# Loading attention keys as whole contiguous rows, shifted by half a row, into a single buffer behind the queries

## The chip, the cores and the metric

The kernel runs on one core of one Trainium2 chip. The metric is the device time of one execution in microseconds (us). Engines are named as in the profile: PE is TensorE (PEld its weight loads), DVE is VectorE, ACT is ScalarE, POOL is GpSimd, and SP is SyncE, whose queue issues nearly all DMAs.

## The reference

What is computed is a pooled attention, followed by a routed feed-forward layer.

```
q, k, v: (8 batches, 8 heads, 1152 rows, 64), float32
q_pool = mean of each two successive query rows          # 576 queries a head
attn   = softmax(q_pool @ k.T / sqrt(64));  x = attn @ v # x: (8, 576, 512), heads side by side
score  = x @ w_gate                                      # one a token
for each batch: the 128 tokens with the highest score get
    x += sigmoid(score) * (relu(x @ w1) @ w2)            # w1: 512 x 1024, w2: 1024 x 512
```

## The kernel before

The work is done by the class `_Plain`; the order of every instruction on every engine is written out by hand in `run` (line 1576), and nothing is rearranged afterwards. A second routine, `_any_scores`, stands behind a branch for inputs out of range and isn't taken here.

Heads are taken in 32 pairs, and each pair in two halves of 288 pooled queries, so that the main loop has 64 rounds, h = 0 to 63. In each round PE computes the scores of half h (`scores`, L883: 36 matmuls of 64x64 weights by 288 columns, four of them for each of nine blocks of keys), and then the weighted values of half h - 1 (`weighted`, L901, 36 matmuls). The profile shows each of these matmuls as two records, hence "x72" for a block. ACT takes the exponents of the scores (L890). POOL (L922) and DVE (L927) sum them into the softmax's denominators, and POOL and DVE also gate, divide and rank. Twice in each pair of batches and once in the end the expert layers run on PE in between (L1451, L1326, L1346).

Each of the pairs 1 to 31 (pair 0 is loaded in another way, by `load_first`) is prepared thus:

- `load_pair` issues eight DMAs on SP's queue. The 1152 key rows of a head are cut into 32 runs of 36 rows, one run to a partition. Four "quarters" (two heads by two halves of the 64 numbers of a row) fill the 128 partitions of the tile kb, so that each DMA (L742) fetches 32 x 36 pieces of 32 numbers, 128 bytes each. The queries go the same way into qb (L745). kb has two buffers, as the pool `load` has by default; qb has one.
- `prepare_pair` adds neighbouring queries on POOL (L767, qb to qp), and DVE turns keys (L770, kb to kT) and queries (L774, qp to qT) in blocks of 32 x 32. kT and qT have two buffers each. L770 frees a kb buffer, L767 frees qb.
- `load_values` issues four DMAs (L756), lines of 2,304 bytes, into one of two buffers of v_sb.

A round with even h = 2n issues `prepare_pair` for pair n + 1. The next round, h = 2n + 1, issues on SP in this order: the loads of keys and queries of pair n + 2, the values of pair n + 1, the stores of a finished pair's x (`stored`, L1038), and a piece of the weights in the early rounds. Behind them, at the marks in `units`, come the routing's small DMAs (L1108 to L1111, L1208, L1212, L1283, L1296), and copies of the summed weights, tw (L725, L730). SP takes its queue strictly in order: where one DMA waits for a buffer, all behind it wait too.

At one place the tile kb serves for something else: the routing of batch 6 borrows one for a 128 x 512 block on its way to a transposition (L1292 to L1298).

Of the kernel before, what the change touches and what calls it, by code (L numbers as in the profile page):

```python
# [10 lines left out]
P = 128  # L11
BLK = 32

G = 3
F32 = mybir.dt.float32
# [12 lines left out]
def _any_scores(  # L28
# [450 lines left out]
    pairs = [(b, hp) for b in range(B) for hp in range(NPAIR)]  # L479
    in_pair = [(j, t) for j in range(2) for t in range(NF)] + [(0, NF)]  # L480
    upcoming = load_pair(*pairs[0])
    run(prepare_pair(upcoming))
    preparing = iter(())
    routing = iter(())
# [23 lines left out]
    for n, (b, hp) in enumerate(pairs):  # L508
        pair = upcoming
        run(preparing)  # L510
        if hp == 0:
            x = xpool.tile([P, NT, Dm], F32, name="x")
        for i, (j, t) in enumerate(in_pair):
            now = {"pair": pair, "j": j, "t": t, "x": x}
            advance(now)
            if two is not None and two["t"] == NF and two["pair"]["hp"] == NPAIR - 1:
                run(routing)
                routing = routed(two["pair"]["b"], two["x"])
            one, two = now, one
            if i == 0 and n + 1 < len(pairs):  # L520
                upcoming = load_pair(*pairs[n + 1])
                preparing = prepare_pair(upcoming)
            if n == 0 and i == 0:
                load_weights()
            if i >= 3:
                next(preparing, None)
            next(routing, None)
    for _ in range(2):
        advance(None)
        one, two = None, one  # L530
    run(routing)
    run(routed(B - 1, x))


class _Plain:
# [199 lines left out]
    def load_pair(self, b, hp):  # L735

        nc = self.nc
        kb = self.load.tile([P, self.KB, BLK], F32, name="kb")
        qb = self.load.tile([P, self.QB, 2, BLK], F32, name="qb", bufs=1)
        for j, ds, rows in self.quarters():  # L740
            of = self.k[b, 2 * hp + j, :, ds]
            nc.sync.dma_start(kb[rows, :, :], of.rearrange("(i n) d -> i n d", i=BLK))  # L742
        for j, ds, rows in self.quarters():
            of = self.q[b, 2 * hp + j, :, ds].rearrange("(i m) d -> i m d", i=BLK)
            nc.sync.dma_start(qb[rows, :, :, :].rearrange("i n r d -> i (n r) d"), of)  # L745
        return {"k": kb, "q": qb, "b": b, "hp": hp}

    def load_values(self, pair):
# [12 lines left out]
    def prepare_pair(self, pair):  # L761

        nc = self.nc
        qp = self.load.tile([P, self.QB, BLK], F32, name="qp", bufs=1)
        kT = pair["kT"] = self.load.tile([P, self.S], F32, name="kT")
        qT = pair["qT"] = self.load.tile([P, self.Sp], F32, name="qT")
        nc.gpsimd.tensor_tensor(  # L767
            out=qp[:, :, :], in0=pair["q"][:, :, 0, :], in1=pair["q"][:, :, 1, :], op=ALU.add
        )
        nc.vector.transpose(  # L770
            kT.rearrange("p (c g i) -> p c g i", c=self.NC, i=BLK),
            pair["k"].rearrange("p (g c) d -> p c g d", c=self.NC),
        )
        nc.vector.transpose(qT[:, :], qp.rearrange("p n d -> p (n d)"))  # L774

# [296 lines left out]
    def routed(self, b, part):  # L1072


        nc, ffn, Sp, NT, NF = self.nc, self.ffn, self.Sp, self.NT, self.NF
# [138 lines left out]
        for s0, w in self.slots:  # L1214
# [64 lines left out]
            if b != self.B - 1:  # L1279

                n = P // BLK
# [7 lines left out]
            if b != self.B - 1:  # L1289
                yield True  # L1290
                if b == self.B - 2:
                    moved = self.load.tile([P, self.KB, BLK], F32, name="kb")  # L1292
                else:
                    moved = ffn.tile([P, NT, P], F32, name="pick", bufs=1)
                moved = moved.rearrange("p t n -> p (t n)")[:, 0 : self.Dm]
                nc.sync.dma_start(moved, copy.rearrange("a (j b) m -> (a j) (b m)", b=n))  # L1296
                yield "sums" if b < self.B - 2 else True
                nc.vector.transpose(  # L1298
                    xeT.rearrange("p c (j b) -> p c b j", b=n),
                    moved.rearrange("p (b i c) -> p c b i", b=n, c=self.ND),  # L1300
                )
            else:
                yield mid
                pv = self.banks()[:, 0, :].rearrange("p (c n) -> p c n", n=P)
                of = xe.rearrange("p (n c) -> p c n", c=self.ND)
                for c in range(self.ND):
                    nc.tensor.transpose(pv[:, c, 0:w], of[0:w, c], self.ident[0:w, 0:w])
                nc.scalar.copy(xeT[:, :, 0:w], pv[:, 0 : self.ND, 0:w])
# [451 lines left out]
```

## Time and profile before

| | us |
|---|---|
| timed runs (3) | 689.4, 690.31, 693.59; median 690.31 |
| the profiled execution | 686.07 |
| its span, from the first to the last instruction | 684.3 |
| DVE transposing keys, L770, 31 times | 42.1 in all, 1.357 each |
| POOL adding queries, L767, 31 times | 43.7 in all, 1.410 each |
| DMA traffic in the span | 101.22 MB, 148 GB/s at the mean |

The page gives for each engine its busy time, its share of the span and its instructions. Below that, rows of 40 digits cut the span into equal slices of 17.1 us, in which a digit is the busy share in tenths (9 is 90% or more). The DMA row is the mean busy share of the core's 16 DMA engines; PEclk is the granted clock of TensorE. A queue's row has its packets, its megabytes, and the share of the 16 engines' span that its packets took. The chain of work that ended last is followed back from the last instruction. In its list by time, and in the timeline, a row is: start, duration, engine, line, and what it writes and reads; a number behind x says how many instructions were merged. In the list of DMA issues the columns are what is written and read, the queue, the number of DMAs, kilobytes of each, and the median time in us from issue to landing. On SP's rows the duration is the time that SP spent on issuing. In PE's rows the weights of a block can be loaded a little ahead of its first matmul.

### The profile page before, as it was taken

Reading aid. Unit: us, or ns where it says so; the run is one execution under the profiler, and the core shown is the slowest. Engines: PE = TensorE matmul, PEld = TensorE weight load, DVE = VectorE, ACT = ScalarE, POOL = GpSimd, SP = SyncE. Lnnn points to the kernel's source line nnn. Section 1 sums busy time; section 2 is a strip of 40 time slices with the busy share of each in tenths; the row PEclk is TensorE's granted clock in tenths of the full one; section 3 lists DMA queues with packets and bytes.
Section 4 is the critical chain, followed back from the end, with each engine's and each line's share of the span. In section 5 each row is a group of like instructions: output and inputs, shape, how many; then the busy total and the mean of one; then the engine's idle time right before and its main releaser. Section 6 shows DMA issues by size and latency. Waiting matters only on the chain.

```text
span 684.3 us, 23659 instructions
## 1 busy us (share of the span) xinstructions
PE 676.4 (99%) x9972; PEld 570.0 (83%) x9972; DVE 531.6 (78%) x844; ACT 457.5 (67%) x998; POOL 516.1 (75%) x503
## 2 busy tenths in 40 slices
PE   8999999999999999999999999999999999999996
PEld 6667899999999998786889899777788999877875
DVE  3867888998999886786599976595879989688830
ACT  5677778777877773847777777583877777575220
POOL 4778888889888883866997888383999798559241
PEclk9999999999999999999999999999999999999999
DMA  8888888778768878743878797773787877544311
GB/s 169 161 178 186 200 149 206 162 133 173 153 147 173 170 146 144 211 87 79 227 133 184 128 191 139 141 184 63 156 192 167 148 152 166 117 116 119 81 47 36
DMA packets 396899, 101.22 MB, mean 148 GB/s; under 512 B 377200, under 2 KB 380912, under 8 KB 395504
## 3 DMA queue, kind: packets, MB, share of 16 engines
q1 hardware_dynamic: 395328, 95.13, 67.3%
q0 software_dynamic: 1296, 4.20, 1.9%
q8 instruction: 80, 1.31, 0.8%
q10 hardware_dynamic: 160, 0.30, 0.2%
q14 instruction: 35, 0.29, 0.1%
HBM read 81.97 MB, written 17.62 MB: 146 GB/s over the span
## 4 chain that ended last, share of the span: by engine, by line
PE 96%; DMA 2%; issue 1%; POOL 0%; ACT 0%; POOLq 0%; DVE 0%
PE ps L901 41%; PE ps L883 41%; PE ps L1451 11%; DMA out_dram<-xe,index 1%; PE ps L1326 1%; PE ps L616 1%; DMA out_dram<-lines,index_part 0%; PE ps L850 0%; PE ps L833 0%; ACT p L890 0%; PE ps L1229 0%; POOL xe L1511 0%; PE ps L1131 0%; POOL out_dram L1393 0%; ACT hT L1334 0%
## 5 line engine op out<-in xcount | busy, mean ns | idle before, releaser
L890 ACT ACTIVATE p<-ps 128x576 f32<-128x576 f32 x576 | 320.4, 699 | 3.0 <-PE ps L883 2.9
L922 POOL TENSOR_TENSOR acc<-p 128x576 f32<-128x576 f32 x192 | 275.5, 1462 | 31.4 <-ACT p L890 30.8
L883 PE MATMUL ps<-qT,kT 64*64 64x288 f32 x4608 | 295.5, 403 | 0.6 <-DVE token L637 0.5
L901 PE MATMUL ps<-p,v_sb 64*64 64x288 f32 x4608 | 295.2, 403 | 0.0
L901 PEld LDWEIGHTS ps<-p,v_sb 64*64 64x64 f32 x4608 | 236.3, 133 | 43.6 <-ACT p L890 12.1
L883 PEld LDWEIGHTS ps<-qT,kT 64*64 64x64 f32 x4608 | 230.9, 133 | 49.1 <-ACT p L890 5.1
L927 DVE TRANSPOSE_TENSOR_REDUCE fold<-p 128x54 f32<-128x1728 f32 x64 | 126.1, 1970 | 43.7 <-ACT p L890 43.4
L927 DVE TRANSPOSE_TENSOR_REDUCE fold<-acc 128x54 f32<-128x1728 f32 x64 | 124.9, 1951 | 22.2 <-POOL acc L922 22.1
L909 ACT COPY two<-ps 128x576 f32<-128x576 f32 x64 | 40.8, 637 | 136.6 <-PE ps L901 126.6
L911 POOL TENSOR_TENSOR av<-two 128x288 f32<-128x288 f32 x64 | 51.2, 800 | 80.7 <-ACT two L909 79.1
L990 POOL TENSOR_TENSOR prod<-avb,w_gate 128x288 f32<-128x288 f32 x64 | 51.1, 800 | 0.2
L767 POOL TENSOR_TENSOR qp<-qb 128x576 f32<-128x576 f32 x31 | 43.7, 1410 | 6.2 <-DMA qb<-in_q_dram 3.4
L980 DVE STREAM_TRANSPOSE avb<-av 128x288 f32<-128x288 f32 x64 | 28.8, 451 | 24.4 <-POOL av L911 24.0
L770 DVE STREAM_TRANSPOSE kT<-kb 128x1152 f32<-128x1152 f32 x31 | 42.1, 1357 | 0.0
L967 ACT ACTIVATE sums<-total,tiny 32x18 f32<-32x18 f32 x124 | 38.2, 308 | 1.9
L1027 POOL TENSOR_TENSOR x<-avb,rec 128x576 f32<-128x576 f32 x30 | 34.8, 1159 | 0.0
L1178 DVE SCALAR_TENSOR_TENSOR pick<-sc_row,gate_sc,before 128x128 f32<-128x128 f32 (+1 forms) x40 | 29.7, 744 | 1.4
L952 ACT COPY groups<-sum 32x36 f32<-32x36 f32 x124 | 27.2, 220 | 1.6
L1049 DVE TENSOR_REDUCE red<-prod 128x9 f32<-128x288 f32 x64 | 27.7, 433 | 0.1
L1459 ACT COPY s<-ps 128x256 f32<-128x256 f32 (+1 forms) x27 | 11.4, 447 | 20.9 <-PE ps L1451 20.9
L937 DVE TENSOR_REDUCE sum<-fold 128x18 f32<-128x108 f32 x64 | 21.9, 342 | 2.2
L1459 ACT COPY hT<-ps 128x512 f32<-128x512 f32 (+1 forms) x15 | 7.8, 544 | 23.3 <-PE ps L1451 21.3
(136 smaller groups left out, 493.1 us busy)
## 6 DMA issues: line engine op xcount, KB each, us to landing
kb<-in_k_dram SPq DMA_DIRECT2D x124, 144.0 KB, 4.3
qb<-in_q_dram SPq DMA_DIRECT2D x124, 144.0 KB, 3.7
v_sb<-in_v_dram SPq DMA_DIRECT2D x124, 144.0 KB, 3.6
tw<-tw SPq DMA_DIRECT2D x10, 1024.0 KB, 7.2
out_dram<-x SPq DMA_DIRECT2D x128, 72.0 KB, 3.2
lines<-row_rank SPq DMA_DIRECT2D x7, 640.0 KB, 4.1
w<-in_moe_w_dram SPq DMA_DIRECT2D x8, 512.0 KB, 5.1
tw<-tw SPq DMA_DIRECT2D x8, 512.0 KB, 4.7
```

Of the source, the lines that this page charges most:

```text
L767: nc.gpsimd.tensor_tensor(out=qp[:, :, :], in0=pair["q"][:, :, 0, :], in1=pair["q"][:, :, 1, :], op=ALU.add)
L770: nc.vector.transpose(kT.rearrange("p (c g i) -> p c g i", c=self.NC, i=BLK), pair["k"].rearrange("p (g c) d -> p c g d", c=self.NC),)
L883: nc.tensor.matmul(sc[keys, j, 0:n], lhsT=pair["kT"][rows, c * P + keys.start : c * P + keys.stop], rhs=pair["qT"][rows, qs], start=True, ...
L890: nc.scalar.activation(p[:, c // G, c % G, :, :], sc[:, :, 0:n], AF.Exp, scale=self.scale)
L901: nc.tensor.matmul(av[j * self.D : (j + 1) * self.D, e, 0:n], lhsT=half["pair"]["v"][keys, j, c, :], rhs=half["p"][keys, c // G, c % G, j, :],
L909: nc.scalar.copy(two[:, :, :], av[:, :, 0:n])
L911: nc.gpsimd.tensor_tensor(out=half["av"][:, :], in0=two[:, 0, :], in1=two[:, 1, :], op=ALU.add)
L922: nc.gpsimd.tensor_tensor(out=acc[:, u, :], in0=units[:, 0, u, :], in1=units[:, 1, u, :], op=ALU.add)
L927: nc.vector.tensor_reduce(fold[:, a, :], of.rearrange("p u (m d) -> p (u m) d", d=BLK), AX.X, ALU.add, apply_transpose=True,)
L967: self.nc.scalar.activation(tot[rows, :], pair["total"][:, j * self.QB : (j + 1) * self.QB], AF.Identity, bias=self.tiny[0:BLK, 0:1],)
L990: self.nc.gpsimd.tensor_tensor(out=pair["prod"][:, ns, :], in0=pair["avb"][:, ns, :], in1=self.w_gate[:, hp : hp + 1, :].broadcast_to([P, ...
L1451: nc.tensor.matmul(args[0], lhsT=args[1], rhs=args[2], start=k == 0, stop=k == n - 1)
```

## The change

Keys: each DMA fetches, for each of the 32 partitions of its quarter, one contiguous line of 36 x 64 - 32 = 2,272 numbers, 9,088 bytes, in place of 36 pieces of 32. For the second half of a row the line begins 32 numbers later, so that in both cases the 32 numbers that are wanted of key row n stand at the beginning of a 64-number slot n of the tile; the other 32 are fetched and not used. The tile kb is twice as wide, 64 numbers for 32, and has one buffer instead of two: the same room. L770 reads the first 32 of each 64.

Order: in `load_pair` the four query DMAs are issued ahead of the four key DMAs. On all other engines the order of instructions is what it was. On SP the first key DMA of a pair now waits for DVE's transposition of the previous pair's keys; the first query DMA waits, as before, for POOL's addition of the previous pair's queries.

The tile that batch 6 borrows takes the new shape and the one buffer, too.

```diff
@@ def load_pair(self, b, hp):
-        kb = self.load.tile([P, self.KB, BLK], F32, name="kb")
+        kb = self.load.tile([P, self.KB, self.D], F32, name="kb", bufs=1)
         qb = self.load.tile([P, self.QB, 2, BLK], F32, name="qb", bufs=1)
-        for j, ds, rows in self.quarters():
-            of = self.k[b, 2 * hp + j, :, ds]
-            nc.sync.dma_start(kb[rows, :, :], of.rearrange("(i n) d -> i n d", i=BLK))
         for j, ds, rows in self.quarters():
             of = self.q[b, 2 * hp + j, :, ds].rearrange("(i m) d -> i m d", i=BLK)
             nc.sync.dma_start(qb[rows, :, :, :].rearrange("i n r d -> i (n r) d"), of)
+        n = self.KB * self.D - BLK
+        for j, ds, rows in self.quarters():
+            of = self.k[b, 2 * hp + j].rearrange("(i n) d -> i (n d)", i=BLK)
+            nc.sync.dma_start(
+                kb[rows, :, :].rearrange("i n d -> i (n d)")[:, 0:n], of[:, ds.start : ds.start + n]
+            )
@@ def prepare_pair(self, pair):
         nc.vector.transpose(
             kT.rearrange("p (c g i) -> p c g i", c=self.NC, i=BLK),
-            pair["k"].rearrange("p (g c) d -> p c g d", c=self.NC),
+            pair["k"][:, :, 0:BLK].rearrange("p (g c) d -> p c g d", c=self.NC),
         )
@@ in routed(self, b, part):
                 if b == self.B - 2:
-                    moved = self.load.tile([P, self.KB, BLK], F32, name="kb")
+                    moved = self.load.tile([P, self.KB, self.D], F32, name="kb", bufs=1)
```

Here BLK is 32, D is 64, KB is 36 and P is 128; `quarters` yields the head j, the half ds of a row, and the 32 partitions.

## The prediction

> **What bounds the kernel now.** I read the page's table of engines first, then the 40 slices, the chain of work that ended last, the DMA issues, and last the timeline of SyncE's queue (SP), DVE, POOL and PE's weight loads, pair by pair.
>
> ```profile
> PE 676.4 (99%) x9972; PEld 570.0 (83%) x9972; DVE 531.6 (78%) x844; ACT 457.5 (67%) x998; POOL 516.1 (75%) x503
> PEclk9999999999999999999999999999999999999999
> DMA  8888888778768878743878797773787877544311
> q1 hardware_dynamic: 395328, 95.13, 67.3%
> ```
>
> TensorE is busy for 676.4 of 684.3 us, at full clock in every slice. The DMA engines are busy 70 to 90% for most of the run; that is no bound until PE is seen waiting for them. An ordinary stretch of the chain:
>
> ```profile
> 102.24 4.36 PE ps L883 x72
> 106.61 4.38 PE ps L901 x72
> 110.99 4.37 PE ps L883 x72
> 115.36 4.37 PE ps L901 x72
> ```
>
> From 19 to 634 us the chain is PE alone: a block of scores (L883), a block of weighted values (L901), 4.36 to 4.38 us each with no gap, whether the slice's DMA digit is 8 or 4. A block that doesn't stretch runs at its own rate. The few longer ones (4.55 at 40.80, 4.47 and 4.52 from 389.75) are worth 0.5 us together, and ScalarE's exponents ended their idle. No PE line in the list of waits names a DMA.
>
> [...]
>
> So a load costs time only if a block finds its operand late. The loads, and the place where they are tightest:
>
> ```profile
> kb<-in_k_dram SPq DMA_DIRECT2D x124, 144.0 KB, 4.3
> qb<-in_q_dram SPq DMA_DIRECT2D x124, 144.0 KB, 3.7
> v_sb<-in_v_dram SPq DMA_DIRECT2D x124, 144.0 KB, 3.6
> tw<-tw SPq DMA_DIRECT2D x10, 1024.0 KB, 7.2
> ```
> ```profile
> 359.14 7.13 SPq L742 DMA_DIRECT2D kb<-in_k_dram  x4
> 366.37 4.54 SPq L745 DMA_DIRECT2D qb<-in_q_dram  x4
> 371.01 2.07 SPq L756 DMA_DIRECT2D v_sb<-in_v_dram  x4
> ```
> ```profile
> 354.93 1.41 POOL L767 TENSOR_TENSOR qp<-qb 128x576 f32<-128x576 f32 x1
> ```
> ```profile
> 357.08 1.36 DVE L770 STREAM_TRANSPOSE kT<-kb 128x1152 f32<-128x1152 f32 x1
> 358.37 0.72 DVE L774 STREAM_TRANSPOSE qT<-qp 128x576 f32<-128x576 f32 x1
> ...
> 374.32 1.36 DVE L770 STREAM_TRANSPOSE kT<-kb 128x1152 f32<-128x1152 f32 x1
> ```
> ```profile
> 363.04 4.36 PEld L883 LDWEIGHTS ps<-qT,kT 64*64 64x64 f32 x72
> ...
> 376.32 3.70 PEld L901 LDWEIGHTS ps<-p,v_sb 64*64 64x64 f32 x64 [0.20 <-ACT p L890]
> ```
>
> Keys and queries are turned at 357.08, done at 359.09, wanted by PE at 363.04: 3.95 us in hand. Over all 31 pairs the same rows give 3.5 us or more, but for 1.3 (the first, done at 21.6), 0.70 and 0.68 (L770 at 342.87 and 508.30). The values are tighter: issued last on SP, to 373.08, plus 3.6 to land is 376.7, and PE takes them at 376.32. By that count the hand is nothing at 376.32 and 211.16, 0.6 at 541.74, 1.9 to 2.2 at 228.63, 246.11 and 576.69, and over 3 elsewhere; as PE doesn't wait, those landed faster than the median.
>
> **The change part by part.**
>
> *Line length.* A pair's keys were 4 x 32 x 36 = 4,608 lines of 128 bytes; they become 128 lines of 9,088. Bytes rise from 31 x 4 x 147,456 = 18.3 MB to 31 x 4 x 290,816 = 36.1 MB, the mean rate from 148 to (101.2 + 17.8) / 684.3 = 174 GB/s; today's slices reach 227. The 142,848 short packets took at most about 18.6 ns each (67.3% x 16 x 684.3 us over q1's 395,328), 24 points of the share; less if short ones are cheaper than the mean. The trace has no 284 KB load. Its landing lies between v_sb's 3.6 us (144 KB in long lines) and tw's 7.2 (1,024 KB), by size 3.6 + 140 x 3.6 / 880 = 4.2, which I take, as the size is nearest v_sb's; today 4.3 at the median, 8.6 at most. SP's issue takes 914 ns at the median for 1,152 lines, 426 for v_sb's 64 (311 at least). I take 0.43: 1.7 us a pair instead of 3.7, with 0.31 and 0.91 as ends. On the path: 0, PE waits for no load.
>
> *Order.* The queries' DMAs go ahead of the keys' on the one SP queue. Their wait for L767 was there before, since qb had one buffer already; now keys, too, stand behind it and behind 4 x 0.86 = 3.4 us of issues. Queries come earlier where L767 isn't the wait. POOL's 3.4 us of waits for qb should shrink; POOL is off the path: 0.
>
> *One buffer for kb.* A pair's first key DMA now waits for the L770 of the pair before. In the stretch shown: L767 ended at 356.34, queries issue from 359.14 to 362.6; L770 ended at 358.44, so the new wait is over before SP gets there; keys issue to 364.3 and land at 368.5, against a want of 374.32. Done for all pairs, the wait is last on SP only twice, where DVE comes late out of routing work (L770 at 269.51 and 434.92): 2.8 and 3.4 us, and what SP issues behind it, values first, then x's stores and the routing's small DMAs, goes 0.1 us later than before (values at 272.6 and 438.0 for 272.46 and 437.87), with over 25 us in hand. From the keys' last issue to their L770 there are 8.75 us at the least (pair 2), 9 to 9.6 in four more, 10 or more elsewhere, for a landing of 4.2. Where L767 is late and SP waits, values come up to 2 us later (73.5 for 71.57) with 11 in hand; in the tight places they come earlier, by 4.0 (211.16), 6.7 (376.32) and 5.0 us (541.74). On the path: 0. If this cover were gone, a late landing would stop DVE at L770, the folds queued behind it, and then PE.
>
> [...] If one buffer meant no overlap, 31 landings of 4.2 us would come out, 130 us. The rows above leave the load room, and the sum has 0.
>
> *The transpose's reading.* L770 reads the same 1,152 elements in runs of 32, now with a gap behind each. No row has just this. Below: 1.36 us as now, since the runs stay whole and successive runs lay apart already; nothing would make it quicker. Above: L1298, which picks elements four apart, 1.11 us for 512, so 2.5 for 1,152. I take 1.36. The upper end puts 36 us on DVE; from 100 to 200, where it is busy for 91.85, it would reach 98.4.
>
> *Start and end.* Pair 1's queries are issued from 5.67 instead of 10.45, its keys from about 10.5 instead of 5.67, landing near 17 before L770's 19.58. The kb tile borrowed at 639 us only has another shape; its last reader ended at 601.9. Both 0.
>
> Sum: 0. The profiled execution took 686.07 us (span 684.3 and 1.8 around it); the timed runs 689.4, 690.31 and 693.59, so it stands 4.2 below their median. Nothing moves on the profile's scale. The one loose end, the values' hand, can only pull the runs toward their fast end, so I say the lowest of them: 689.4.
>
> **The rivals.**
>
> 1. *Relief makes it faster.* For: values land just in time in three places. Against: PE doesn't wait there. If all that sets the median above the profiled run were such waits, 686.1; with PE's idle of the first 20 us (2.0), 684.1, still only 0.9% under the median.
>
> 2. *DVE reads the wider pitch more slowly.* Against: whole runs. Price at the upper end: 0.45 + 0.47 us in the two pairs with 0.7 in hand, and up to 5.7 pairs x 1.15 = 6.6 in the stretch where DVE is full: 686.07 + 7.5 = 693.6, or 697 on the runs' scale (from 689.4); halfway, 693.
>
> 3. *The long lines hold up SP, and values come late: slower.* Place: the values behind the keys. Point: four key issues take over 1.7 + 4.0 = 5.7 us, after which PE waits at 211.16. Price: if they take 8.7, today's longest four (at 279.25), 7.0 beyond my 1.7, the hands of ten tight pairs run out by 3.0, 1.6, 1.4, 0.8, 0.7, 0.6, 0.4, 0.2 and two noughts, 8.7 in sum: 694.8, or 699 on the runs' scale (690.31 + 8.7), 1.3% slower. For: twice the bytes in a queue that is 67% full. Against: tw's loads of 1,024 KB issue in 0.58 us at the median and land in 7.2.
>
> 4. *The long lines are cut up on the way*, so that one costs what two of today's do. Time as forecast until rival 3's point.
>
> **How the numbers follow.** About 1% is what a measurement of this kernel can tell from no change. Hidden: 0.78, and rival 4 0.04. Rival 2: 0.07, nearly all within 1%. Rival 3: 0.07, slower. Rival 1: 0.04, counted as faster by over 1% for the part that the profile can't show. So 0.04 faster, 0.89 within, 0.07 slower. The range: from 684.1 (rival 1) to 696.0, between rival 2's middle and its end; rival 3 lies above.
>
> **What would show it.** Right: blocks of 4.37 us, PE near 676 busy, about 139,000 packets fewer, q1 near 113 MB, key issues under 0.5 us, landing near 4.2, an SP wait for L770 in a few pairs. Wrong: L770 above 1.4 us, DVE waiting for kb, or a PE wait at L883 or L901 released by L770, L774 or a DMA.

## The result and the profile after

The changed kernel takes 714.1 us at the median of six runs (711.48 to 720.93), the kernel before 691.38 (689.4 to 693.68): a ratio of 1.0331, 95% interval 1.0295 to 1.0366. The forecast was 689.4, "the same", with 696.0 as the upper end of its range. The profiled execution took 711.59 us, with a span of 709.8 where before it was 684.3: 25.5 us more. The lines of after stand three lower in the code: scores L886, weighted values L904, the transpositions L773 and L777, the addition L770, the stores of x L1041; L742 is now the queries and L746 the keys, L759 the values.

The page of after, the rows on engines, DMA and chain, and two groups (the columns of a group: busy us in all and mean ns of one, then the idle time just before them and what ended most of it):

```profile
PE 687.2 (97%) x9972; PEld 564.5 (80%) x9972; DVE 531.6 (75%) x844; ACT 458.0 (65%) x998; POOL 515.4 (73%) x503
DMA  9889899898879887873887988786678989844310
q1 hardware_dynamic: 256448, 112.91, 73.3%
PE 67%; DMA 12%; POOL 8%; SPq 5%; DVE 4%; issue 3%; ACT 2%; POOLq 0%; DVEq 0%; ACTq 0%
L904 PE MATMUL ps<-p,v_sb 64*64 64x288 f32 x4608 | 303.3, 408 | 9.5 <-DMA v_sb<-in_v_dram 9.3
L886 PE MATMUL ps<-qT,kT 64*64 64x288 f32 x4608 | 299.7, 406 | 6.0 <-DVE qT L777 5.4
```

The same two groups before:

```profile
L883 PE MATMUL ps<-qT,kT 64*64 64x288 f32 x4608 | 295.5, 403 | 0.6 <-DVE token L637 0.5
L901 PE MATMUL ps<-p,v_sb 64*64 64x288 f32 x4608 | 295.2, 403 | 0.0
```

The 25.5 us are 14.7 in which PE stands idle (709.8 - 687.2 = 22.6, before 684.3 - 676.4 = 7.9) and 10.8 in which it is busy for longer with the same 9,972 matmuls. The idle time lies at the two waits that the groups name: 9.5 us ahead of L904 (before 0.0), nearly all of it for the values' DMA, and 6.0 ahead of L886 (before 0.6). The same two lines are busy for 8.1 and 4.2 us more (before 295.2 and 295.5); neighbouring groups overlap at their edges, so that the two don't add up to the 10.8. The chain, PE alone before, now runs through DMA and SP's queue for 17% of the span.

The DMA issues of after, and then what SP waited for longest (us in total, times, longest):

```profile
kb<-in_k_dram SPq DMA_DIRECT2D x124, 284.0 KB, 6.6
qb<-in_q_dram SPq DMA_DIRECT2D x124, 144.0 KB, 4.2
v_sb<-in_v_dram SPq DMA_DIRECT2D x124, 144.0 KB, 7.5
out_dram<-x SPq DMA_DIRECT2D x128, 72.0 KB, 5.1
```
```profile
SPq L1041 <- DMA kb<-in_k_dram: 80.9, 105, 2.1
SPq L742 <- POOL qp L770: 44.0, 10, 8.7
```

A key load lands 6.6 us after its issue at the median (before 4.3). But DMAs that did not change land late, too: the values 7.5 us after theirs (before 3.6), the stores of x 5.1 (before 3.2). And the 128 stores on SP's queue waited 105 times for a key load to land, a wait that the trace of before does not have at all; it delays all that SP issues behind them. In all 105, the load that was waited for is the eighth DMA ahead of the store on SP's queue: with four loads of keys, four of values and four stores in this order, a key load has that place. The stores of before:

```profile
out_dram<-x SPq DMA_DIRECT2D x128, 72.0 KB, 3.2
```

What that makes of one pair, first SP's queue in the kernel before, then after:

```profile
123.12 4.14 SPq L742 DMA_DIRECT2D kb<-in_k_dram  x4
127.35 4.24 SPq L745 DMA_DIRECT2D qb<-in_q_dram  x4
131.69 2.58 SPq L756 DMA_DIRECT2D v_sb<-in_v_dram  x4
```
```profile
117.42 5.33 SPq L1041 DMA_DIRECT2D out_dram<-x  x4
...
128.94 4.36 SPq L742 DMA_DIRECT2D qb<-in_q_dram  x4
133.40 2.46 SPq L746 DMA_DIRECT2D kb<-in_k_dram  x4
135.95 1.83 SPq L759 DMA_DIRECT2D v_sb<-in_v_dram  x4
```

The issue of keys takes 2.46 us instead of 4.14, as was meant. Yet SP comes to this pair 5.8 us later than before, and to the values 4.3 us later (135.95 for 131.69). The chain of after shows the rest, values last, and then PE's timeline at this place and at the next such one:

```profile
137.35 7.67 DMA v_sb<-in_v_dram
```
```profile
136.94 4.63 PE L886 MATMUL ps<-qT,kT 64*64 64x288 f32 x72
144.30 6.88 PE L904 MATMUL ps<-p,v_sb 64*64 64x288 f32 x70 [2.73 <-DMA v_sb<-in_v_dram]
...
219.13 6.83 PE L904 MATMUL ps<-p,v_sb 64*64 64x288 f32 x70 [2.18 <-DMA v_sb<-in_v_dram]
...
565.41 6.31 PE L904 MATMUL ps<-p,v_sb 64*64 64x288 f32 x70 [3.19 <-DMA v_sb<-in_v_dram]
```

PE had ended its scores at 141.57 and stopped for 2.73 us, until the values began to be there; the last of their four loads, issued at 137.35, took 7.67 us, to 145.02, and most of the block follows it. The block behind the stop takes 6.88 us instead of 4.63. The stretches around it say why (us, busy time and instructions of PE, PEld, DVE, ACT and POOL, then the granted clock, the DMA share and GB/s):

```profile
144.30:150.00 5.70, 5.55 (x56) 3.60 (x60) 5.59 (x17) 0.06 (x1) 0.95 (x2) 0.70 0.77 129
150.00:155.00 5.00, 5.00 (x86) 3.83 (x81) 4.93 (x10) 3.48 (x7) 1.55 (x3) 1.00 0.99 228
```

The granted clock is 0.70 in the 5.7 us after the stop, and 1.00 thereafter. So this stop costs twice: 2.73 us of standing, and some 2.4 of slow matmuls. The three blocks shown are 6.88 + 6.83 + 6.31 - 3 x 4.5 = 6.5 of PE's 10.8 us of longer busy time (4.5 is 70 records at the rate of a block of 72 in 4.63). The two other stops of over 2 us stand ahead of scores:

```profile
359.38 6.28 PE L886 MATMUL ps<-qT,kT 64*64 64x288 f32 x72 [2.69 <-DVE qT L777]
531.40 4.60 PE L886 MATMUL ps<-qT,kT 64*64 64x288 f32 x72 [2.25 <-DVE qT L777]
```

The first has 1.7 us more of slow matmuls behind it (granted clock 0.73 over these 6.28 us, and 0.75 over each of the blocks at 219.13 and 565.41), which makes 8.2 of the 10.8. The second has none: the granted clock is 1.00 from 531.40 to 536.00, after a stop longer than the 2.18 ahead of 219.13. So a stop of this length does not always cost twice. At 359.38 the chain runs back through POOL to the routing's indirect loads (7.17 us there; 6.7 at the median, before 4.0), so values and keys are not the only loads that came late.

### The profile page after: what moved, and what is told of

The parts are those of the page before. It is cut to its first block, busy times and chain, and to the rows that moved or that the text cites. A ratio compares the mean times of both kernels' runs of the same rounds, so it can differ in the third digit from the quotient of the medians.

```text
span 709.8 us, 23676 instructions
## 1 busy us (share of the span) xinstructions
PE 687.2 (97%) x9972; PEld 564.5 (80%) x9972; DVE 531.6 (75%) x844; ACT 458.0 (65%) x998; POOL 515.4 (73%) x503
## 2 busy tenths in 40 slices
DMA packets 258019, 119.00 MB, mean 168 GB/s; under 512 B 234352, under 2 KB 238064, under 8 KB 252656
## 3 DMA queue, kind: packets, MB, share of 16 engines
q1 hardware_dynamic: 256448, 112.91, 73.3%
## 4 chain that ended last, share of the span: by engine, by line
PE 67%; DMA 12%; POOL 8%; SPq 5%; DVE 4%; issue 3%; ACT 2%; POOLq 0%; DVEq 0%; ACTq 0%
PE ps L904 30%; PE ps L886 25%; PE ps L1454 11%; POOL acc L925 4%; DMA v_sb<-in_v_dram 4%; DMA kb<-in_k_dram 2%; DMA out_dram<-xe,index 2%; DVE fold L930 2%; SPq L742 2%; SPq L746 2%; ACT p L893 1%; DMA row<-total 1%; PE ps L1329 1%; DMA xe<-out_dram,index 1%; POOL x L1030 1%
## 5 line engine op out<-in xcount | busy, mean ns | idle before, releaser
L904 PE MATMUL ps<-p,v_sb 64*64 64x288 f32 x4608 | 303.3, 408 | 9.5 <-DMA v_sb<-in_v_dram 9.3
L886 PE MATMUL ps<-qT,kT 64*64 64x288 f32 x4608 | 299.7, 406 | 6.0 <-DVE qT L777 5.4
L904 PEld LDWEIGHTS ps<-p,v_sb 64*64 64x64 f32 x4608 | 235.5, 135 | 62.5 <-ACT p L893 14.8
L886 PEld LDWEIGHTS ps<-qT,kT 64*64 64x64 f32 x4608 | 228.2, 133 | 61.6 <-ACT sums L970 5.9
L773 DVE STREAM_TRANSPOSE kT<-kb 128x1152 f32<-128x1152 f32 x31 | 42.1, 1360 | 16.4 <-DMA kb<-in_k_dram 7.0
L770 POOL TENSOR_TENSOR qp<-qb 128x576 f32<-128x576 f32 x31 | 43.7, 1410 | 0.9 <-DMA qb<-in_q_dram 0.9
```

The costliest lines, as they stand in the source:

```text
L770: nc.gpsimd.tensor_tensor(out=qp[:, :, :], in0=pair["q"][:, :, 0, :], in1=pair["q"][:, :, 1, :], op=ALU.add)
L773: nc.vector.transpose(kT.rearrange("p (c g i) -> p c g i", c=self.NC, i=BLK), pair["k"][:, :, 0:BLK].rearrange("p (g c) d -> p c g d", c=s ...
L886: nc.tensor.matmul(sc[keys, j, 0:n], lhsT=pair["kT"][rows, c * P + keys.start : c * P + keys.stop], rhs=pair["qT"][rows, qs], start=True, ...
L904: nc.tensor.matmul(av[j * self.D : (j + 1) * self.D, e, 0:n], lhsT=half["pair"]["v"][keys, j, c, :], rhs=half["p"][keys, c // G, c % G, j, :],
```

## The experiments

Two theories were tried against each other. The bytes: twice as many for the keys, written by each DMA into only 32 partitions, keep the DMA engines busy, so that what stands behind them lands late. The queue: the order of issue and the one buffer make SP wait, with the values behind. Later runs split the first: width of the destination, length of the lines, the shift by half a row, and the neighbours in the queue. Each ratio is to the kernel before, timed again beside the run (medians from 686.14 to 692.12 us).

**The order alone, with the short lines and two buffers.**

```diff
-        for j, ds, rows in self.quarters():
-            of = self.k[b, 2 * hp + j, :, ds]
-            nc.sync.dma_start(kb[rows, :, :], of.rearrange("(i n) d -> i n d", i=BLK))
         for j, ds, rows in self.quarters():
             of = self.q[b, 2 * hp + j, :, ds].rearrange("(i m) d -> i m d", i=BLK)
             nc.sync.dma_start(qb[rows, :, :, :].rearrange("i n r d -> i (n r) d"), of)
+        for j, ds, rows in self.quarters():
+            of = self.k[b, 2 * hp + j, :, ds]
+            nc.sync.dma_start(kb[rows, :, :], of.rearrange("(i n) d -> i n d", i=BLK))
```

> The kernel before with only the order changed: queries ahead of keys, keys still in 128-byte lines and two buffers. Theory A (the long lines keep the DMA engines busy for longer, and the values, which are queued behind them, come late): no key line is longer, so about 691 us, within 1% of before, values landing about 3.6 us after issue. Theory B (the waits on SP: keys behind the queries, and behind the transposition that frees the one buffer): part of the loss is here, 697 to 705. Theory C (not the bytes, but that the long lines are issued in 0.42 us each, so that values enter the queues right behind a burst): about 691.

Measured: 1.015 (1.0099 to 1.02). The queries, now in front, meet their wait for POOL's addition undelayed: 46.3 us in 9 waits; before, the keys' issue filled most of that time, and 10.3 us in 4 waits were left. SP's waits in this kernel, and its queue at the place shown above:

```profile
SPq L742 <- POOL qp L767: 46.3, 9, 12.0
```
```profile
127.55 5.21 SPq L742 DMA_DIRECT2D qb<-in_q_dram  x4
132.80 4.82 SPq L745 DMA_DIRECT2D kb<-in_k_dram  x4
137.72 2.08 SPq L756 DMA_DIRECT2D v_sb<-in_v_dram  x4
```

Values are issued at 137.72, later even than in the changed kernel, but they land in 3.5 us at the median, and PE stops for them for only 0.57 us here. Values issued 6.0 us later than before were nearly covered by the hand; the changed kernel, with values issued 1.8 us earlier than here, stops for longer, since its last load lands in 7.67.

**One buffer alone**: keys first, short lines.

```diff
-        kb = self.load.tile([P, self.KB, BLK], F32, name="kb")
+        kb = self.load.tile([P, self.KB, BLK], F32, name="kb", bufs=1)
```

> The kernel before with one buffer for kb and nothing else: keys still ahead of queries, 128-byte lines. Keys first with one buffer was the slowest with long lines (1.053), because SP waits for the transposition with keys, queries and values behind it. If that holds for short lines too: 698 to 712 us, with an SP wait of 40 us or more at the key load for DVE's L770. If it takes the long lines to make it hurt: 687 to 694.

Measured: 1.0207 (1.0187 to 1.0227). SP waits for DVE's transposition, and PE for values:

```profile
SPq L742 <- DVE kT L770: 57.2, 17, 8.8
```
```profile
PE ps L901 <- DMA v_sb<-in_v_dram: 10.7, 9, 3.0
```

**Order and one buffer together**, short lines: both edits above.

> Queries ahead of keys and one buffer for kb, but the old 128-byte lines: everything of the change except the line. Theory A: about 691 us, within 1%. Theory B: the whole loss, 711 to 717. Theory C: about 691.

Measured: 1.0082 (1.005 to 1.0113), less than one buffer alone; against the order alone the intervals overlap. With one buffer the queries in front are of use, since their issue fills the time until the keys' buffer is free: of the 57.2 us that SP waited for the transposition, one wait of 2.6 is left under that name, and 13.3 us in all under DVE's. The theory of the queue holds with the short lines, but explains about a quarter of the 3.3%.

**The order undone in the changed kernel**: keys first, long lines, one buffer.

> The changed kernel with only the order undone: keys ahead of queries, long lines and one buffer kept. The order alone cost 1.5% with short lines and two buffers, 0.8% with one. If the parts add, the time is 704 to 709 us. If all the loss is bytes, it stays at 711 to 717. If the order is what lets the bytes hurt, because the values then stand right behind the long lines: 692 to 700, with values landing at 5 us or less.

Measured: 1.0526 (1.0505 to 1.0548), above all three ranges. SP waits 58.5 us for the transposition in 14 waits, with all the rest behind it. That is no more than in one buffer alone (57.2), which lost 2.1%. What is new is that the queries, now right behind the long lines, take SP 228.8 us to issue in all, for 124.9 there and 131.5 in the change; among SP's seven longest waits, down to 11.0 us in all, no store waits for a key load. So, inside the change, the order saves two points rather than costing any.

**The long lines at the old bytes**: 4,608 bytes to a line, tile as wide as before; with the order and the one buffer of the change.

```diff
-        n = self.KB * self.D - BLK
+        n = self.KB * BLK
```

> The changed kernel with contiguous lines of 4,608 bytes in place of 9,088, so that a key DMA moves as many bytes as before the change (147,456), in 32 lines; order and the one buffer as in the change. It reads only the first half of the key rows and takes them for all, so keys and output are others. Theory A in its form 'bytes': 691 to 695 us, values landing 4 to 5 us after issue, q1's share at or below 67%. Theory A in its form 'a long line itself is slow': between, 698 to 708. Theory B: 714. Theory C: 705 to 714, since the burst is issued as fast as in the change.

Measured: 0.9974 (0.9942 to 1.0005). The page's rows:

```profile
PE 676.5 (99%) x9972; PEld 564.8 (82%) x9972; DVE 530.5 (77%) x844; ACT 457.7 (67%) x998; POOL 517.1 (76%) x503
q1 hardware_dynamic: 256448, 95.13, 61.4%
kb<-in_k_dram SPq DMA_DIRECT2D x124, 144.0 KB, 3.8
v_sb<-in_v_dram SPq DMA_DIRECT2D x124, 144.0 KB, 4.1
```

This is the run that decides. Long lines, order and one buffer together cost nothing that can be measured: PE is busy for 676.5 us as before, no DMA stops it, and with quick issues the 0.8% of order and one buffer is gone as well. What is left of the change is the 17.8 MB of numbers that nobody uses. Loaded as the change loads them, in four DMAs into 32 partitions each, they make the whole of the loss; the next runs load them in other ways.

**The destination wide**: the same bytes, in four DMAs of 128 partitions by 2,272 bytes in place of 32 by 9,088.

```diff
-        n = self.KB * self.D - BLK
-        for j, ds, rows in self.quarters():
+        n = (self.KB * self.D - BLK) // 4
+        for c in range(4):
...
-                kb[rows, :, :].rearrange("i n d -> i (n d)")[:, 0:n], of[:, ds.start : ds.start + n]
+                kb.rearrange("p n d -> p (n d)")[:, c * n : (c + 1) * n], of[:, at : at + n]
```

> The changed kernel with the same bytes of keys in the same number of DMAs, but each DMA writes a quarter (2,272 bytes) of all 128 partitions' lines, instead of whole lines of 32 partitions. It takes other key rows than the reference, so the output is another. Theory A1 (twice the bytes cost, in whatever form): 708 to 716 us, values landing about 7.5 us after issue, q1's share about 73%. Theory A2 (long lines are slow because a DMA writes into only 32 partitions): q1's share at 66% or less, values landing at 5 us or less, 688 to 698. Theory A3 (the odd length and the shift of 128 bytes): like A1, since these lines are odd too.

Measured: 1.0123 (1.0088 to 1.0158). The time is in the range of theory A2; its other marks, a share of 66% at most and values within 5 us, came out at 66.7% and 6.0.

```profile
q1 hardware_dynamic: 268352, 112.91, 66.7%
kb<-in_k_dram SPq DMA_DIRECT2D x124, 284.0 KB, 6.1
v_sb<-in_v_dram SPq DMA_DIRECT2D x124, 144.0 KB, 6.0
```

**Its counterpart: lines cut as short, destination narrow.** Each line of the change in four pieces of 2,176 bytes.

```diff
-        n = self.KB * self.D - BLK
+        n = 9 * self.D - BLK
...
-            of = self.k[b, 2 * hp + j].rearrange("(i n) d -> i (n d)", i=BLK)
+            of = self.k[b, 2 * hp + j].rearrange("(i m r) d -> i m (r d)", i=BLK, r=9)
```

> The changed kernel with each line cut in four: nine rows less half a row, 2,176 bytes, still four DMAs into 32 partitions each, 4% fewer bytes (what is left out is never read). The wide lines of 2,272 bytes differed from the change both in the length of a line and in the number of partitions written. Theory 'narrow' (32 partitions to write to): q1's share 70 to 73%, 706 to 713 us, values landing about 7 us after issue. Theory 'length' (a DMA engine is slow on lines of some 9 KB): q1's share 65 to 68%, 692 to 700, values landing at 6 us or less.

Measured: 1.0252 (1.019 to 1.0314), with 4% fewer key bytes than the change. The time is in the range of theory 'narrow' and the share just above it; the values land in 6.2 us, not 7.

```profile
q1 hardware_dynamic: 268352, 111.39, 73.6%
kb<-in_k_dram SPq DMA_DIRECT2D x124, 272.0 KB, 5.8
```

**One wide DMA with the long lines**: 128 lines of 9,088 bytes at once.

```diff
+        of = self.k[b, 2 * hp : 2 * hp + 2].rearrange("j s d -> (j s d)")[0:n]
+        of = dataclasses.replace(of, ap=[[n // 2, P], [1, n]])
+        nc.sync.dma_start(kb.rearrange("p n d -> p (n d)")[:, 0:n], of)
```

> The changed kernel with one DMA of 128 lines of 9,088 bytes into all 128 partitions, instead of four into 32; the lines overlap in the source by half, so that the same bytes are read and written, but the key rows are not the reference's, and the output is another. Theory 'narrow': q1's share at 67% or less, 688 to 700 us. Theory 'length': q1's share 72% or more, 706 to 716. Three fewer DMAs on SP's queue a pair are worth 1.3 us of SP's time in both.

Measured: 1.005 (1.0021 to 1.0079).

```profile
q1 hardware_dynamic: 254960, 112.90, 66.7%
kb<-in_k_dram SPq DMA_DIRECT2D x31, 1136.0 KB, 8.1
v_sb<-in_v_dram SPq DMA_DIRECT2D x124, 144.0 KB, 7.3
```

These three and the change make a table of two by two, in the time that q1's packets take on all 16 engines (q1's share times the span):

| | lines of 9,088 bytes | lines of 2.2 KB |
|---|---|---|
| 32 partitions to a DMA | 520.3 us (the change) | 519.5 us |
| 128 partitions to a DMA | 466.2 us | 463.2 us |

With the old bytes in long lines it was 61.4% of 684.8, or 420.5 us. So 17.8 MB more cost 99.8 us of all 16 engines when written narrow, and all of the keys' 36.1 MB written wide take 54.1 to 57.1 us less than narrow; the length of the lines makes little difference here. (The 42.7 to 45.7 by which wide lies above 420.5 are not the price of 17.8 MB: in the run with the old bytes the keys' 18.3 MB were still written narrow.) In time, 1.0252 against 1.0123 differ by the width alone (and by 4% of the keys' bytes, which favours the slower).

How the engine time becomes PE's time is not shown as clearly. The values' landing goes with the length of the lines ahead, not with the width: 7.5 and 7.3 us behind 9,088 bytes, 6.2 and 6.0 behind the short ones. Yet PE waits for values 9.3 and 9.8 us with the narrow destinations, 3.3 and 0 with the wide ones. At the place shown above the wide ones issue the values earlier, from 133.30 (short lines) and 127.95 (long) for 135.95, and this can decide as much as the landing. With the one wide DMA there are also three issues fewer to a pair; its PE waits 7.8 us in two places for turned queries.

The one wide DMA also bears on the stores' waits for key loads: with one key load to a pair there are 26, a quarter of the 105 (60.5 us in all), and in the order of issue that load is the eighth DMA ahead of the last of the four stores alone.

**No shift**: lines of 9,216 bytes that begin on whole rows.

```diff
-                kb[rows, :, :].rearrange("i n d -> i (n d)")[:, 0:n], of[:, ds.start : ds.start + n]
+                kb[rows, :, :].rearrange("i n d -> i (n d)")[:, 0:n], of[:, 0:n]
```

> The changed kernel with whole lines of 9,216 bytes and no shift for the second half of d: all else as in the change. The second half of d gets the first half's numbers, so the output is another. Theory A1: 711 to 718 us, q1's share 73 to 74%. Theory A2: the same. Theory A3 (the odd length or the shift makes the lines slow): 690 to 702, q1's share under 70%.

Measured: 1.0382 (1.0355 to 1.0409), with q1 at 73.2% and key landings of 6.6 us, where the shifted lines had 73.3% and 6.6. The shift costs nothing here.

**Neighbouring DMAs in other partitions**: `quarters` yields 0-31, 64-95, 32-63, 96-127.

```diff
-        for j in range(2):
-            for e in range(2):
+        for e in range(2):
+            for j in range(2):
```

> The changed kernel with the four quarters in another order, so that two successive DMAs write the partitions 0-31 and 64-95, then 32-63 and 96-127, instead of 0-31, 32-63, 64-95, 96-127 (the loop is shared by the loads of keys and queries, the stores and ACT's spreading of sums). If long lines are slow because a DMA in flight has only 32 partitions to write to, and another one in flight on other partitions can use what it leaves free: 695 to 709 us, q1's share 68 to 72%. If each DMA is as slow by itself wherever its neighbours write: 711 to 717 us, q1's share 73%.

Measured: 1.0316 (1.029 to 1.0343), q1 at 72.4%, values landing in 6.8 us: hardly a change.

> The kernel before with the same new order of quarters. PE has no wait for a load in the profile of before, so 0.995 to 1.005 of its time on either theory; a gain beyond that would mean that timed runs do wait for loads.

The same in the kernel before: 1.0008 (0.9994 to 1.0023).

**Values ahead of the next pair's loads**, in the changed kernel: `load_values` before `load_pair` in `run`.

> The changed kernel, but with the values of a pair issued ahead of the next pair's queries and keys on SP. Theory A: PE's waits for values (9.3 us in five places) go, and with them the matmuls that run slowly after a stop; what is left is the waits for kb and qb. 695 to 703 us, values landing near 4 us. Theory B: the waits for L773 and L770 on SP are still there, 711 to 717. Theory C: like A.

Measured: 1.0222 (1.0165 to 1.0279). No wait for values is left, and PE now waits for the turned queries:

```profile
PE ps L886 <- DVE qT L777: 9.1, 7, 3.4
```

It gives back a third of the loss; the queue is as full as before (q1 at 74.1%), and what stands last on it is late.

> The kernel before with one step moved: the values of a pair are issued ahead of the next pair's keys and queries. By my reading of the profile before, values are the load with the least time in hand there; if timed runs wait for them now and then, this gives 684 to 687 us. If keys and queries get late in their turn, as the changed kernel with values first showed (waits at the scores for the turned queries), 690 to 697.

The same in the kernel before: 1.0038 (1.0023 to 1.0052). Where no value is late, moving them up gains nothing; PE now waits 3.0 us in four places for turned queries. None of these kernels is faster than the one before; the best, with the old bytes, has an interval that includes 1. Long lines with two buffers of the double width were not run.

## Why the prediction was wrong, point by point

**What bounds the kernel**: right. PE was the bound, with blocks that do not stretch, and the values were the load in the least hand. That the DMA share was "no bound until PE is seen waiting for them" was true of the kernel before, and was then taken for a property of the change.

**Line length: the step that failed.** The prediction put the landing of the keys at 4.2 us, and "On the path: 0, PE waits for no load". Keys landed in 6.6, near the upper of its bounds, 3.6 and 7.2; DVE waited for them 7.0 us in three places. Whether that alone would have stopped PE, no run shows; the step never asked what the loads behind the keys would do. The values' landing was carried over from before at 3.6 us into every later count; it was 7.5. In the tight places, with nothing to 2 us in hand by the prediction's own list, 3.9 us more is a stop. One row was a hint: the digits of 7 and 8 in the DMA row, for a queue to which the change gave 19% more bytes (112.91 MB for 95.13). The packets saved are real (258,019 in all, 138,880 fewer), but by the run with the old bytes they are worth 40.0 us of the 16 engines (460.5 - 420.5), while the bytes cost 99.8. The prediction priced the packets at up to 24 points of the share, 164 us, and the bytes at nothing.

**Issue of the keys**: right at the median, 0.42 us each for an estimate of 0.43. The four took more at the place shown, 2.46 us for 1.7.

**Order**: "0" was wrong with short lines, where it costs 1.5% alone; inside the change it is worth two points, by the run with keys first. SP's arrival at each pair was read off the trace of before, with key issues made shorter. A wait that is met undelayed, and the stores' waits for key loads (80.9 us in all, which no row of before showed), push all later arrivals. Where the prediction had values "in the tight places" come "earlier, by 4.0 (211.16)", PE stopped for 2.18 us at the same block, at 219.13 in the new trace.

**One buffer**: the wait on SP was small as predicted, if more frequent than twice; the key issues waited 10.4 us in all for DVE, in 19 waits of 1.9 at most. The 2.1% of one buffer alone, against 0.8% with the order, shows that the order is its cover: the prediction's stretch has the queries' issue ahead of the wait, but it priced the two edits one by one. The 130 us that it worked out for no overlap at all did not come: giving up the second buffer alone, where nothing covers it, cost 2.1%, 14.8 us at the medians.

**The transposition's reading**: right. 1.360 us against 1.357, so rival 2 falls.

**The rivals.** Rival 3 had the right place, "the values behind the keys", and the right sign, at 0.07. Its mechanism was SP's issue time, with four issues of over 5.7 us as its point; they took 1.7 us at the median, and values were late all the same, through the landing and the stores' waits. Its price of 8.7 us was a third of what came, since it counted stops only: there were 14.7 us of idle time and 10.8 of longer busy time. Rival 1 has nothing to show for it even with the old bytes (684.8 us of span). Rival 4, lines cut up, falls: q1's packets fell by 138,880, just 31 x (4,608 - 128), so each line counts as one packet. And cut in four by hand, the lines cost the same engine time.

**Signs**: the packets, the 113 MB and the key issues came as said; PE "near 676 busy" and "landing near 4.2" failed. On its list of what would prove it wrong were a PE wait for a DMA or for L777's queries, and DVE waiting for kb; all three came (9.3, 5.4 and 7.0 us). The two long waits for queries, at 359.38 and 531.40, came where it had counted pairs with the least in hand, 0.70 and 0.68.

**What the width costs.** Narrow, 17.8 MB in 99.8 us are 178 GB/s; at that rate the keys' 36.1 MB take 202 us, by estimate, and 54.1 to 57.1 us less make 244 to 249 GB/s wide. Alternating the quarters, so that 0-31 and 64-95 follow each other, moved q1's share by 0.9 points only (72.4% for 73.3%). That the narrow destination is the cause is shown by the runs of two widths; by what mechanism it costs, no run shows.

**What a stop costs beyond its length.** At four of the five stops the granted clock stood at 0.50 for 3.4 us: from 145.35 to 148.75, 220.44 to 223.85, 360.39 to 363.79 and 565.19 to 568.59, and at 1.00 from there to the end of each block. By estimate, half the clock for 3.4 us makes 1.7 us of longer matmuls; the four blocks were 1.7 to 2.4 us longer. The four stops were of 2.73, 2.18, 2.69 and 3.19 us; after the one of 2.25 the clock did not fall, so that the length of the stop alone doesn't decide.

Open is why SP holds a store until the eighth DMA ahead of it has landed, how much of the 3.3% this wait makes and how much the late landing, and 2.6 of PE's 10.8 us of longer busy time, which were not followed block by block.

## What to carry to other kernels

Try long lines where they bring no more bytes: here they saved 40 us of DMA engine time, and doubling the keys' bytes into 32 partitions cost 100. When a load grows, count again the landing of every load that stands behind it, take the hand of the last one issued as the budget, and carry a queue's lateness on from round to round instead of reading its arrivals off the old trace. A stop of PE can cost more than its length, for the slow clock that may follow: 1.7 to 2.4 us more here after four of five stops of 2.2 to 3.2 us, and nothing after the fifth. When issues on a queue get quicker, look also at which load each later DMA is held for; here it was the eighth ahead.

## What the runs showed of the hardware

- Engine time of the same traffic differed with the partitions that one DMA of keys writes: 520.3 us over 32 and 466.2 over 128 with lines of 9,088 bytes, 519.5 and 463.2 with 2.2 KB.
- Between lines of 2.2 KB and of 9,088 bytes the length mattered little to the engine time (the same figures; the 519.5 are for 1.5 MB less), and neither did a start in the middle of a row matter (q1's share 73.3% with it, 73.2% without). The values behind them landed 1.3 us later with the long lines (7.5 for 6.2 us narrow, 7.3 for 6.0 wide).
- Four stops of PE of 2.18 to 3.19 us came with 3.4 us at a granted clock of 0.50, which began between 0.2 us before the end of the stop and 1.3 us behind it; one of 2.25 us was followed by a clock of 1.00.
- A store on SP's queue was held 105 times until the key load eight DMAs ahead of it had landed, where such loads took 6.6 us; 26 times where only one of four stores had a key load in that place, and where keys stood elsewhere no such wait is among SP's longest (keys first, down to 11.0 us in all; values first, down to 4.5).
- The 124 issues of queries took SP 228.8 us in all right behind the long lines (keys first), for 131.5 ahead of them (the change).
